# A fused attention and mixture-of-experts kernel: squared rows summed on GpSimd, bias steps for both sides at once, routing counts by rounding, and a written list of all steps

## The chip, the cores and the metric

The kernel runs on one core of one Trainium2 chip. The metric is the device time of one execution in microseconds (us), taken as the median of several runs. The profile is a trace of one execution; the lines "L503" and the like are lines of the kernel before. Engines are TensorE (PE, with its weight loads PEld), VectorE (DVE), ScalarE (ACT), GpSimd (POOL) and SyncE (SP), which issues most transfers; the others run in parallel and are tied by semaphores, and each works through its own instructions in the order in which the program gives them.

## The reference

Attention by random features, then one expert per token. There are 8 batches, 8 heads, 576 tokens, 64 dimensions, 128 features, 8 experts:

```
phi(x):  proj = x @ omega.T            # x scaled by 64**-0.25
         h = proj - sum(x*x)/2
         return exp(h - max(h)) / sqrt(128)
kv  = phi(k).T @ v ; z = sum(phi(k))
att = (phi(q) @ kv) / (phi(q) @ z + 1e-6)          # [4608, 512] in all
logits = att @ w_gate ;  e = argmax(logits)
gate = softmax(logits)[e] ; eom = sigmoid(att @ w_output_gate)[e]
out  = gate * eom * (relu(att @ w1[e]) @ w2[e])
```

The sum of squares of a token is the same for all its features, so it cancels against the maximum up to rounding; the kernel forms it all the same.

## The kernel before, in words

**Units.** The attention is cut into 32 units, four chunks of tokens (1152 tokens of two batches each) by eight heads. A unit loads k and q transposed (`xt32`, 576 KB) and values (`rawv`, 325 KB), and from unit 8 on k and q in natural order too (`xn`, 576 KB). It projects both sides (steps `pp`, three groups of 3 x 128 tokens, L503), takes the least value of each token (`mx`, L525, DVE), makes a bias from it (`nb`, L531, or L534 and L538), and takes the exponential with that bias (`ex`, L544, ACT). Then come the product of keys and values (`kv`, L640), halves of it in f16 (`kvs`, L660), its product with the gate weights (`kt`, `kg`, L678, L683), the transposed q features (`tq`/`th`/`tl`, L594, L599, L601 in the first eight units, a transposing DMA later), the numerator and denominator (`pn`, L714), the division (`xf`, L723 to L727) and two halves for the store (`xh`, L744, DVE; `xl`, L748, POOL). The gate logits are added up over the heads (`lga`, L766, POOL).

**The sum of squares.** In the first eight units ("whole" ones, `u < WHOLE`) the projection is in f32: `squares` writes the squares of the transposed data into `xn` (L480, POOL; L478, ACT for unit 0), and each group of `pp` adds six more matmuls for each six of the projection, squares times a tile `half` that holds a constant, so that PSUM holds projection and squares together. The bias is then one DVE instruction for each side and group (L531). From unit 8 on the projection is in f16 halves (`xhi`, `xlo`), ACT squares the natural data (`sqa`, L443), DVE sums it over the 64 dimensions (`sqr`, L448), and the bias is two instructions for each side and group (L534, L538).

**Routing and items.** When the eight heads of a chunk are done, `route`, `counts`, `ranks`, `places`, `gates` and `weigh` choose an expert and a place for each token, and `table`, `assign`, `lists`, `controls`, `pid`, `gi`, `advance` form lists of 128 tokens of one expert each ("items"). These are chains of small DVE instructions on 8 to 144 columns (L840 to L1189), with matmuls for the counts (L891 to L901) and lists (L1151). A rank is cut into slot and place by a cast to integer, a shift by 7 and a cast back. An item gathers its rows (`gx`, L1458, an indirect DMA from POOL), transposes them by DMA (`xt`, L1470), and runs the two layers (`hA`, `hB`, L1495, and `out`, L1526, PE, with `relu` L1502 ACT and `rest` L1506 DVE), scales (`os`, ACT) and stores (`put`, POOL). 38 items carry tokens here; where the expert changes, 4 MB of weights are brought and cut into halves (`sw`, L365 ACT, L369 DVE). The weights of a first expert, guessed, are cut early (`w0h`, `w0l`, the same lines).

**What sets the order.** All steps are registered with `plan.add`. A planner (`Plan.order`) plays them through once: of the ready steps it takes the one with the lowest rank among those that can start earliest, by costs that are written beside each step, with a model of DMA, of PSUM banks in two classes (5 for attention, 3 for items) and of TensorE at half speed after a quiet stretch. The result is the order of instructions on every engine; across engines semaphores hold.

Of the kernel before, what the change touches and what calls it, by code (L numbers as in the profile page):

```python
# [31 lines left out]
KEY = 64  # L32
KC = DM // P
# [40 lines left out]
SHIFT = {'hi': -1.4, 'lo': 0.3, 'sqa': 1.9, 'sqr': 2.3, 'T': 1.8, 'pp': 0.1, 'mx': 0.5, 'nb': -0.4, 'ex': -2.0, 'eh': -0.7, 'el': 1.4, 'eT': 0.4, 'kv': -0.5, 'kvs': -1.6, 'pn': -0.1, 'xf': -0.9, 'xh': 0.1, 'xl': 0.7, 'xT': -3.4, 'rows': -0.1, 'lg': -2.2, 'lga': -1.4, 'route': -1.8, 'gx': 1.7, 'xt': 1.0, 'hA': 0.7, 'hB': -1.1, 'relu': -2.1, 'rest': -0.6, 'out': 0.3, 'os': -0.1, 'put': 1.0}  # L74
# [25 lines left out]
C_END = C_DOWN + 1  # L100


def constants():
# [6 lines left out]
    c[:, C_ITEM:C_PART] = np.arange(NITEM)  # L110
# [4 lines left out]
    c[FEW:, C_DOWN] = -float(FEW)  # L115
    c[:, C_BOTH + 1 : C_UPPER : 2] = np.arange(NSC * NC) * P
# [3 lines left out]
    m[:, 2, :] = np.arange(P)  # L120
    m[:, 3, :] = np.eye(P)
    return c, m, np.eye(P, dtype=np.float32)


class Plan:

    HANDOFF, DRAIN, DMA_START, DMA_END, DMA_TURN, BACKLOG, LATE = 0.19, 0.13, 0.65, 0.95, 0.3, 2.5, 2.5
    TICK, ENOUGH = 3.413, 3060.0

    def __init__(self, banks):
        self.steps, self.seq, self.banks, self.bank_of = {}, 0, banks, {}
        self.part = 0
        self.makers, self.readers, self.bufs = {}, {}, {}  # L140

    def add(
        self, key, engine, cost, fn, after=(), rank=0.0, tiles=(), bank=None, frees=(), dma=0.0, turn=False, early=None, cols=None,
        lead={},
    ):


        assert key not in self.steps, key
        cost = cost if isinstance(cost, tuple) else (cost,) * len(engine)
        bank = [] if bank is None else bank if isinstance(bank, list) else [bank]  # L150
        s = dict(key=key, eng=engine, cost=cost, fn=fn, after=list(after), rank=(rank + SHIFT.get(key[0], 0.0), self.seq), bank=bank)
        s.update(frees=frees, dma=dma, turn=turn, tiles=sorted(set(tiles)), early=early, part=self.part, lead=lead)
        s["cols"] = cost[0] * 2400.0 if cols is None else cols
        self.seq += 1
        self.steps[key] = s
        for tag, i in s["tiles"]:
            self.readers.setdefault((tag, i), []).append(key)
# [18 lines left out]
    def lag(self, a, b):  # L176

        if a == b:
            return 0.0 if a == ("PE",) else self.DRAIN
        return 0.06 if b == ("SP",) else self.HANDOFF  # L180

    def order(self):
        steps = self.steps
        users, missing = {}, {}
        for k, s in steps.items():
            deps = set(s["after"])
            for tag, i in s["tiles"]:
                deps |= set(self.readers.get((tag, i - self.bufs[tag]), ()))
            s["deps"] = deps
            missing[k] = len(deps)  # L190
            for d in deps:
                assert d in steps, (k, d)
                users.setdefault(d, []).append(k)
        free_at = {"SP": 0.6, "DVE": 0.9, "POOL": 0.7, "ACT": 1.9, "PE": 0.1}
        bank_free = {b: 0.0 for b in range(sum(self.banks.values()))}
        bank_cls, b0 = {}, 0
        for c, n in self.banks.items():
            bank_cls[c] = range(b0, b0 + n)
            b0 += n
        bank_cls["e"] = range(b0)  # L200
        dma_free = 0.0
# [4 lines left out]
        while ready:  # L206
            best = None
            for k in ready:
# [9 lines left out]
                if best is None or t < best:  # L218
                    best = t
# [1462 lines left out]
```

## Time and profile before

| what | before |
|---|---|
| median of 3 runs (lowest to highest) | 659.51 us (658.62 to 664.33) |
| the profiled execution's own time | 659.44 us |
| its span (first to last instruction) | 657.6 us |
| matmul instructions | 8732 |
| DVE instructions busy | 1277 |
| read from and written to HBM | 83.86 MB, 19.30 MB |

The profile gives, for each group of instructions of one line and operation, the time during which it was busy, the mean duration of one, and the idle time of the engine before it with what ended it. Instructions of one engine overlap in their pipelines, so the mean of one is longer than its pitch (the distance from start to start); a table of windows gives the busy time of an engine without counting twice.

### The profile page before, as it was taken

What the parts mean: (1) busy time and instruction counts of PE and PEld (TensorE: products, weight loads), DVE (VectorE), ACT (ScalarE), POOL (GpSimd) and SP (SyncE); (2) the same over time, 40 slices, a digit from 0 to 9 for tenths busy, and PEclk for the clock granted to TensorE, in tenths of its full rate; (3) what the DMA queues carried; (4) which work ended last, traced back from release to release, by engine and by line L of the source; (5) the groups of instructions that cost most, each with busy time, mean ns of one, the idle gap of its engine ahead of it and who ended that gap; (6) DMA issues with size and microseconds to landing.
All of it is one profiled execution on the core that took longest, in us unless ns stands there. A gap on an engine that the chain in (4) does not pass through costs nothing. (4 is left out here: it accounts for less than half of the span.)

```text
span 657.6 us, 22358 instructions
## 1 busy us (share of the span) xinstructions
PE 608.3 (93%) x8732; PEld 474.6 (72%) x8732; DVE 426.8 (65%) x1277; ACT 412.0 (63%) x970; POOL 342.7 (52%) x235
## 2 busy tenths in 40 slices
PE   6999986799999899899989999999999999999983
PEld 6899975677777677677757777877768677677763
DVE  4899889876877897567697876752783430251043
ACT  5886797689888859788875788772521521341151
POOL 1343545569956958879574788955222122121202
PEclk9999988799999999999999999999999999999998
DMA  9544588998999989978999485867945846834460
GB/s 316 204 136 139 165 295 206 257 250 193 300 270 283 240 230 210 226 195 243 298 278 212 100 205 132 130 105 182 291 103 182 219 92 154 255 61 102 153 225 15
DMA packets 145894, 129.09 MB, mean 196 GB/s; under 512 B 104270, under 2 KB 127440, under 8 KB 144464
## 3 DMA queue, kind: packets, MB, share of 16 engines
q1 hardware_dynamic: 139760, 107.45, 64.6%
q0 software_dynamic: 5984, 19.72, 9.2%
q8 instruction: 85, 1.39, 0.9%
q14 instruction: 65, 0.53, 0.3%
HBM read 83.86 MB, written 19.30 MB: 157 GB/s over the span
## 5 line engine op out<-in xcount | busy, mean ns | idle before, releaser
L1495 PE MATMUL ph<-xt,w1h 128*128 128x128 f16 (+1 forms) x2432 | 206.1, 218 | 3.5 <-issue 1.7
L1495 PE MATMUL ph<-xt,w1l 128*128 128x128 f16 (+1 forms) x1216 | 201.4, 217 | 2.2 <-DVE w1l L369 0.9
L1495 PEld LDWEIGHTS <-w1h 128*128 128x128 f16 x2432 | 181.9, 98 | 12.3 <-issue 5.8
L544 ACT ACTIVATE ef<-pp,nb 128x128 f32<-128x128 f32 x576 | 162.9, 392 | 42.0 <-DVE nb L538 33.1
L1506 DVE SCALAR_TENSOR_TENSOR hl<-ph,hh 128x512 f16<-128x512 f32 (+1 forms) x76 | 50.6, 666 | 121.9 <-ACTq L1424 74.9
L567 POOL TENSOR_TENSOR es<-ef,es 128x1152 f16<-128x1152 f32 x44 | 104.9, 2392 | 36.0 <-ACT es L565 21.1
L525 DVE TENSOR_REDUCE pp<-pp 128x3 f32<-128x384 f32 x192 | 102.7, 557 | 30.0 <-PE pp L503 26.2
L1495 PEld LDWEIGHTS <-w1l 128*128 128x128 f16 x1216 | 118.6, 98 | 2.9 <-issue 1.5
L1458 POOL DMA_INDIRECT gx<-rows,gi x38 | 39.9, 1049 | 138.0 <-ACT os L1581 103.1
L1526 PE MATMUL po<-w2h,hl 128*128 128x512 f16 x280 | 106.7, 381 | 2.4 <-DVEq L1424 1.3
L1526 PE MATMUL po<-w2h,hh 128*128 128x512 f16 x280 | 107.1, 382 | 0.0
L1526 PE MATMUL po<-w2l,hh 128*128 128x512 f16 x280 | 106.6, 381 | 0.0
L1502 ACT ACTIVATE hh<-ph 128x512 f16<-128x512 f32 (+1 forms) x76 | 44.3, 583 | 87.5 <-PE ph L1495 71.3
L1526 PEld LDWEIGHTS <-hh 128*128 128x128 f16 x560 | 51.7, 99 | 57.1 <-issue 2.7
L1581 ACT ACTIVATE os<-po,gx 128x512 f32<-128x512 f32 (+1 forms) x36 | 24.5, 682 | 65.6 <-PE po L1526 63.7
L437 POOL TENSOR_TENSOR xlo<-xt,xhi 128x1152 f16<-128x1152 f32 x24 | 57.2, 2385 | 13.5 <-ACT xhi L430 12.2
L565 ACT CAST es<-ef 128x1152 f16<-128x1152 f32 x44 | 51.3, 1177 | 6.3 <-DMA et<-es 5.9
L714 PE MATMUL pn<-kvs,et 128*128 128x81 f16 (+1 forms) x960 | 46.4, 205 | 7.7 <-DVE kvs L701 2.1
L1526 PEld LDWEIGHTS <-hl 128*128 128x128 f16 x280 | 27.5, 98 | 36.0 <-DVE hl L1506 1.9
L714 PEld LDWEIGHTS <-et 128*128 128x128 f16 (+1 forms) x960 | 40.1, 102 | 16.5 <-issue 5.6
L748 POOL TENSOR_TENSOR xs<-xf,xs 128x576 f16<-128x576 f32 x32 | 43.2, 1351 | 10.2 <-DVE xs L744 9.3
L503 PE MATMUL pp<-omh,xhi 64*128 64x128 f16 x432 | 42.6, 221 | 6.3 <-DVE xf L727 3.1
(185 smaller groups left out, 1048.6 us busy)
## 6 DMA issues: line engine op xcount, KB each, us to landing
r<-w SPq DMA_DIRECT2D x10, 2048.0 KB
xt<-kqt SPq DMA_DIRECT2D x32, 576.0 KB
xn<-kqn SPq DMA_DIRECT2D x24, 576.0 KB
rawv<-v SPq DMA_DIRECT2D x32, 325.0 KB
rows<-xs SPq DMA_DIRECT2D x16, 576.0 KB
r<-w SPq DMA_DIRECT2D x8, 512.0 KB
ef<-w SPq DMA_DIRECT2D x2, 512.0 KB
et<-w SPq DMA_DIRECT2D x2, 512.0 KB
```

What stands on the lines that cost most here:

```text
L437: lambda t0=t0, t1=t1: nc.gpsimd.tensor_tensor(out=xl(u)[:, t0:t1], in0=xt32(u)[:, t0:t1], in1=xh(u)[:, t0:t1], op=ALU.subtract),
L503: nc.tensor.matmul(banks["pp", 2 * u + i, g][:, c, :], x[r, t], w[r, :], start=(a == 0), stop=(a == len(ops) - 1))
L525: nc.vector.tensor_reduce(out=pp[:, 3, 0:3], in_=pp[:, 0:3, :], op=ALU.min, axis=AX.X)
L544: nc.scalar.activation(ef(n)[:, c, :], banks["pp", n, g][:, c % 3, :], AF.Exp, bias=nb(n)[:, c : c + 1], scale=-SK)
L565: nc.scalar.copy(es(slot_es(n))[:, 0], ef(n))
L567: nc.gpsimd.tensor_tensor(out=es(slot_es(n))[:, 1], in0=ef(n), in1=es(slot_es(n))[:, 0], op=ALU.subtract)
L714: nc.tensor.matmul(pn[lo:hi, c - c0, :], a[:, c, lo:hi], w[:, b, :], start=(i == 0), stop=(i == len(ops) - 1))
L748: nc.gpsimd.tensor_tensor(out=x[:, :, P + o : P + o + D], in0=xf(u)[:, :, 0:D], in1=x[:, :, o : o + D], op=ALU.subtract)
L1495: nc.tensor.matmul(ph[:, f4, 0:w_], w[qd][:, kk, fo : fo + P], xt(n)[:, x, 0:w_], start=(a == 0), stop=(a == 3 * KC - 1))
L1502: nc.scalar.activation(hh(n)[:, sl, 0:w_], banks["ph", n, g][:, :, 0:w_], AF.Relu)
L1506: nc.vector.scalar_tensor_tensor(out=hl(n)[:, sl, 0:w_], in0=banks["ph", n, g][:, :, 0:w_], scalar=0.0, in1=hh(n)[:, sl, 0:w_], op0=ALU.ma ...
L1526: nc.tensor.matmul(po, x(n)[:, f, :], w[f // 2][:, f % 2, :], start=(f == 0 and a == 0), stop=(f == FC - 1 and a == 2))
```

## The change

**Squares.** The matmuls with `half` are gone. Every unit loads `xn` in natural order. Unit 0 squares it on ACT and sums it on DVE as later units do. Units 1 to 7 form the squares on POOL (1152 columns) and fold them there: 576, 288 and 144 columns of additions, then a scaling of 144 columns; DVE sums the last eight for each token (18 sums out of 144 columns).

**Bias.** `nb` now holds both sides. After the two `mx` of a group, two DVE instructions make the bias of k and q together (6 columns). The exponentials of k wait for the `mx` of q as well.

**Routing.** Counts and ranks are kept as tokens less 63.5, and a rank is rounded to whole slots by adding and subtracting 1.5 * 2^23 * 128; the counts so far come in by two more f32 matmuls (`ident` times `cnt`); several copies are gone. For one chunk and its list the DVE chain has 23 instructions where it had 29 in `ranks` (4, now 3), `places` (5, now 4), `table` (9, now 7), `assign` (8, now 7) and `lists` (3, now 2); the copy `cp` has moved from `lists` into `places`.

**Order.** The planner, its ranks and the table of shifts are gone. `ORDER` lists all 3333 steps by number and `BANKS` the PSUM bank of each use, any of the eight. A number is the place of a step's `plan.add` call: 0 to 30 are constants and first weights, 31 to 85 are unit 0, then 59 steps for each of the units 1 to 7, 51 for each of 8 to 11, 55 for each of 12 to 31, 1803 on the stores of rows, 1819 on the routing, 1906 on the lists and flags, 2112 on the items (16 steps each for the first 25, then 29). So 2118 is the first layer of item 0 (`hA`), 2116 its gather, 1824 `counts` of chunk 0, 710 to 712 `pp` of unit 12, 659 to 661 `pp` of unit 11, 683 and 684 `kv` of unit 11.

```diff
+ORDER = """
+31 0 32 86 87 5 36 34 37 33 1 7 39 38 40 35 45 41 95 89 51 42 43 44 2 146 145 10 4 13 52 98 53 99 54 46 47 48 90 55 49
...
+1807 631 813 670 671 675 676 677 873 634 761 2118 672 678 683 2119 679 667 673 684 874 2120 635 636 710 711 685 637
...
     def order(self):
-        steps = self.steps
...
+        numbered = list(self.steps.values())
+        out = [numbered[int(x)] for x in ORDER.split()]
...
+    def squares(u, R):
+
+        if u == 0:
+            natural_sums(u, R, ("ACT",))
+            return
+        x = lambda: sqt(u)
+
+        def fold(w):
+            if w == D:
+                nc.gpsimd.tensor_tensor(out=x(), in0=xn(u), in1=xn(u), op=ALU.mult)
+            elif not w:
+                nc.gpsimd.tensor_scalar(x()[:, :, :, 0 : D // 8], x()[:, :, :, 0 : D // 8], SK * SK / 2.0, None, ALU.mult)
+            else:
+                nc.gpsimd.tensor_tensor(out=x()[:, :, :, 0:w], in0=x()[:, :, :, 0:w], in1=x()[:, :, :, w : 2 * w], op=ALU.add)
+
+        after = [("ld", "n", u)]
+        for w, cost in ((D, 2.3), (D // 2, 1.2), (D // 4, 0.7), (D // 8, 0.4), (0, 0.3)):
+            plan.add(
+                ("sqa", u, w), ("POOL",), cost, lambda w=w: fold(w), after=after, rank=R - 15, tiles=[("xn", u), ("sqt", u)]
+            )
+            after = [("sqa", u, w)]
+        plan.add(
+            ("sqr", u), ("DVE",), 0.3,
+            lambda: nc.vector.tensor_reduce(
+                out=sqs(u).rearrange("p i c -> p c i"), in_=x()[:, :, :, 0 : D // 8], op=ALU.add, axis=AX.X
+            ),
...
                 if whole:
-                    ops = [(xt32(u), omf), (xsq(), half)]
+                    ops = [(xt32(u), omf)]
...
-            before_ = [("lo", u, x), ("const", "omh")]
+            before_ = [("ld", "t", u) if whole else ("lo", u, x), ("const", "omh")]
...
+        spare = lambda g, at: banks["pp", 2 * u, g][:, 3, at : at + 6].rearrange("p (i c) -> p i c", i=2)
+
+        def least(i, g):
+            nc.vector.tensor_reduce(
+                out=spare(g, 0)[:, i], in_=banks["pp", 2 * u + i, g][:, 0:3, :], op=ALU.min, axis=AX.X
+            )
+
+        def bias(g):
+            c = slice(3 * g, 3 * g + 3)
+            sq = sqs(u)[:, :, c]
+            nc.vector.scalar_tensor_tensor(
+                out=spare(g, 6), in0=spare(g, 0), scalar=SK, in1=sq, op0=ALU.mult, op1=ALU.add
+            )
+            yield
+            nc.vector.scalar_tensor_tensor(
+                out=nb(u)[:, :, c], in0=spare(g, 6), scalar=LIFT, in1=sq, op0=ALU.add, op1=ALU.subtract
+            )
...
-        nc.tensor.matmul(pos[:, 0:NC, :], tri, one, start=True, stop=False)
+        nc.tensor.matmul(pos[:, 0:NC, :], ident, cnt.unsqueeze(1).broadcast_to([P, NC, NE]), start=True, stop=False)
+        nc.tensor.matmul(pos[:, 0:NC, :], tri, one, start=False, stop=False)
...
-        ri = inner(j, "ri", [NC], I32)
-        nc.vector.tensor_copy(ri, rank)
-        yield
-        nc.vector.tensor_scalar(ri, ri, 7, None, ALU.arith_shift_right)
-        yield
-        nc.vector.tensor_copy(key, ri)
-        yield
-        nc.vector.scalar_tensor_tensor(out=rank, in0=key, scalar=-float(P), in1=rank, op0=ALU.mult, op1=ALU.add)
...
+        nc.vector.tensor_scalar(key, rank, ROUND, ROUND, ALU.add, ALU.subtract)
+        yield
+        nc.vector.tensor_tensor(out=rank, in0=rank, in1=key, op=ALU.subtract)
```

More of the change, by code (lines that the diff above doesn't have):

```diff
@@ new lines, in order @@
+        numbered = list(self.steps.values())
+        out = [numbered[int(x)] for x in ORDER.split()]
+        assert len(out) == len({s["key"] for s in out}) == len(numbered)
+        done, taken, free = set(), iter(BANKS.replace("\n", "")), set(range(8))
+        for s in out:
+            before = set(s["after"])
+            for tag, i in s["tiles"]:
+                before |= set(self.readers.get((tag, i - self.bufs[tag]), ()))
+            assert before <= done, s["key"]
+            done.add(s["key"])
+            for _, name, _ in s["bank"]:
+                self.bank_of[name] = int(next(taken))
+                free.remove(self.bank_of[name])
+            for name in s["frees"]:
+                free.add(self.bank_of[name])
@@ L459, in unit @@
         whole = u < WHOLE
-        for nm, t, src, rank in (("t", xt32, kqt, R - 30), ("n", xn, kqn, R - 22))[: 1 if whole else 2]:
+        for nm, t, src, rank in (("t", xt32, kqt, R - 30), ("n", xn, kqn, R - 22)):
             plan.add(
@@ new lines, in unit @@
+                ("pp", u, g), ("PE",), 0.66 if whole else 0.6, lambda g=g: project(g), after=before_, rank=R,
+                tiles=[("xt32", u)] if whole else [("xhi", u), ("xlo", u)],
+                bank=[(cls, ("pp", 2 * u + i, g), [4, M]) for i in range(2)], cols=1536.0 if whole else 1152.0,
+            )
+        spare = lambda g, at: banks["pp", 2 * u, g][:, 3, at : at + 6].rearrange("p (i c) -> p i c", i=2)
[3 more added lines that the diff above has]
+            )
@@ new lines, in unit @@
+        for g in range(G):
+            for i in range(2):
+                plan.add(
+                    ("mx", 2 * u + i, g), ("DVE",), 0.47, lambda i=i, g=g: least(i, g), rank=R + 0.5 * i,
+                    after=[("mx", 2 * u, g)] if i else [("pp", u, g)],
+                )
+            plan.chain(
+                ("nb", u, g), ("DVE",), (0.1, 0.1), lambda g=g: bias(g), rank=R + 0.5,
+                after=[("mx", 2 * u + 1, g)] + [("sqr", u)], tiles=[("nb", u), ("sqs", u)],
+            )
+            for i in range(2):
+                plan.add(
+                    ("ex", 2 * u + i, g), ("ACT",), 0.76, lambda i=i, g=g: exps(i, g), after=[("nb", u, g)], rank=R + i,
+                    tiles=[("nb", u), ("ef", 2 * u + i)], frees=[("pp", 2 * u + i, g)],
@@ L968, in table @@
         t["off"] = off
-        nc.vector.tensor_tensor(out=off[:, 0, :], in0=done[:, 0, :], in1=start, op=ALU.subtract)
+        nc.vector.scalar_tensor_tensor(
+            out=off[:, 0, :], in0=done, scalar=ROUND, in1=start, op0=ALU.subtract, op1=ALU.subtract
+        )
         yield
```

284 lines of the change are left out of this document (83 added, 201 removed), and 127 rows, old and new, of the table ORDER.

## The prediction

> **What bounds the kernel now.** I read the page's first lines, then a table of windows, then TensorE's and VectorE's instructions in order of time in the stages that the change touches, then groups and waits.
>
> ```profile
> span 657.6 us, 22358 instructions
> PE 608.3 (93%) x8732; PEld 474.6 (72%) x8732; DVE 426.8 (65%) x1277; ACT 412.0 (63%) x970; POOL 342.7 (52%) x235
> ```
>
> TensorE is busy for 93% of the span, so at first sight its work is the time. The windows (columns: length, busy time of PE, PEld, DVE, ACT, POOL, granted clock, DMA share, GB/s) say more:
>
> ```profile
> 0.00:10.00 10.00, 4.91 (x46) 4.91 (x48) 2.21 (x10) 3.38 (x7) 2.31 (x5) 1.00 0.83 284
> 10.00:80.00 70.00, 69.32 (x945) 63.14 (x945) 62.20 (x175) 56.86 (x180) 26.89 (x19) 1.00 0.54 177
> 80.00:131.00 51.00, 38.52 (x534) 33.66 (x531) 46.46 (x188) 38.78 (x112) 26.50 (x19) 0.83 0.94 253
> 131.00:440.00 309.00, 294.72 (x4689) 225.31 (x4688) 232.69 (x748) 243.96 (x571) 236.80 (x152) 0.99 0.88 217
> 440.00:640.00 200.00, 193.27 (x2385) 141.39 (x2385) 77.10 (x153) 64.67 (x98) 46.34 (x41) 1.00 0.64 168
> 640.00:657.60 17.60, 7.60 (x150) 6.19 (x146) 6.16 (x7) 4.32 (x7) 3.86 (x2) 0.79 0.06 15
> ```
>
> Up to 80 us, the eight whole units, TensorE never pauses, but VectorE is at 62.20 of 70 and ACT at 56.86. From 80 to 131 TensorE has 12.5 us idle and a clock of 0.83, while VectorE is at 46.46 of 51: it closes chunk 0 and serves the next units. The first item starts at 131:
>
> ```profile
> 115.37 1.16 POOL L1458 DMA_INDIRECT gx<-rows,gi  x1 [0.32 <-DVE rt L1121]
> 130.93 0.27 PE L1495 MATMUL ph<-xt,w1h 128*128 128x128 f16 x2
> ```
>
> After that TensorE is bound by its work: 495.6 of 526.6 us up to the end. So two things set the end: when the items can start, which hangs on VectorE, and how much TensorE work and idle time is left then. TensorE work taken out before 131 us counts only as far as the start of the items moves with it.
>
> **The squares.** Rows of one whole unit (start, duration):
>
> ```profile
> 44.84 2.48 PE L640 MATMUL kv<-rawv,ef 128*128 128x130 f32 x20
> ...
> 48.23 0.39 PE L503 MATMUL pp<-half,xn 64*128 64x128 f32 x4
> 48.45 0.39 PE L503 MATMUL pp<-omf,xt 64*128 64x128 f32 x4
> ...
> 74.08 2.48 PE L640 MATMUL kv<-rawv,ef 128*128 128x130 f32 x20
> ```
>
> From `kv` to `kv` three units take 29.24 us, 9.75 each. One burst with `half` has a pitch of 0.22 us; nine a unit are 2.0 us, 16 us for eight units. TensorE alone would then need 7.75 us a unit. The same three units by engine:
>
> ```profile
> sum 29.24, PE 29.24 PEld 26.75 DVE 27.01 ACT 20.29 POOL 11.93; mean PE 9.75 PEld 8.92 DVE 9.00 ACT 6.76 POOL 3.98
> ```
>
> VectorE has 9.00 us in the 9.75. It becomes the bound, and it gets more: the sum of 144 columns, 0.32 us by the row of that shape in the lists (0.2 to 0.3 as a pitch; I take 0.30). The bias of whole units stays at two instructions a group.
>
> ```profile
> L1002 DVE TENSOR_REDUCE rt<-rt 128x18 f32<-128x144 f32 x1 | 0.3, 316 | 0.0
> L480 POOL TENSOR_TENSOR xn<-xt 128x1152 f32<-128x1152 f32 x7 | 15.1, 2153 | 26.8 <-DMA xt<-kqt 26.8
> L748 POOL TENSOR_TENSOR xs<-xf,xs 128x576 f16<-128x576 f32 x32 | 43.2, 1351 | 10.2 <-DVE xs L744 9.3 <-DVEq L1419 0.4 <-DVE nb L531 0.4
> L766 POOL TENSOR_TENSOR lga<-lga,xf 128x144 f32<-128x144 f32 x24 | 14.2, 590 | 38.9 <-DVE xf L727 22.3 <-DVE nb L538 5.8 <-DVE nb L531 5.5
> L764 POOL COPY lga<-xf 128x144 f32<-128x144 f32 x4 | 1.4, 343 | 4.7 <-DVE xf L727 4.7
> ```
>
> GpSimd's chain: 2.15 for 1152 columns, 1.35 for 576, about 0.9 for 288 (between 1.35 and 0.59), 0.59 for 144, 0.34 for the scaling: 5.3 us instead of 2.15. A unit then has 3.98 + 3.2 = 7.2 us of GpSimd in 9.75, so the chain is covered if it runs a unit ahead; queued behind it are `xl` and `lga` of the unit before, for whose rows and logits nobody waits until chunk 0 closes. But GpSimd and VectorE disturb each other:
>
> ```profile
> 26.49 2.10 POOL L480 TENSOR_TENSOR xn<-xt 128x1152 f32<-128x1152 f32 x1
> 26.54 2.40 DVE L744 CAST xs<-xf 128x576 f16<-128x576 f32 x1
> ...
> 47.00 0.60 DVE L744 CAST xs<-xf 128x576 f16<-128x576 f32 x1
> ...
> 58.15 1.28 POOL L748 TENSOR_TENSOR xs<-xf,xs 128x576 f16<-128x576 f32 x1
> 58.55 1.96 DVE L369 SCALAR_TENSOR_TENSOR w2l<-r,w2h 128x1024 f16<-128x1024 f32 x1
> ...
> 63.55 1.21 DVE L369 SCALAR_TENSOR_TENSOR w2l<-r,w2h 128x1024 f16<-128x1024 f32 x1
> ...
> L744 DVE CAST xs<-xf 128x576 f16<-128x576 f32 x32 | 30.4, 949 | 0.2
> ```
>
> A cast that takes 0.60 us undisturbed took 2.40, until GpSimd's instruction was over; its mean is 0.95, so it waits 0.35. An instruction that meets another at random waits, on average, the sum of the squared lengths over twice the period: (2.15² + 1.28² + 0.59²) / 19.5 = 0.34, which fits. With the new chain the squares sum to 9.7, over 19.5 it is 0.50: 0.16 more. Two VectorE instructions a unit are of this kind, the cast and one weight piece `w0l` (1.96 beside GpSimd, 1.21 without): +0.3. VectorE then needs 9.00 + 0.30 + 0.3 = 9.6 of 9.75 us. The 16 us of TensorE work are covered almost whole; what can be won is VectorE's idle time in this stage, 7.8 us from 10 to 80, of which its new work takes 8 x 0.6 = 4.8. I take **-3**; ends -5 (no new waits: 7.8 less 8 x 0.3) and, with GpSimd always in the way, a rival below. The Trainium skill, page "SBUF — State Buffer", section "Who interferes with whom", calls this an exclusive lock of a port pair, held for a whole instruction, for casts and for VectorE instructions with two SBUF inputs, and says that reductions never take part; the rows above agree for cast and weight piece. By that rule the new sum (`sqr`) never waits, and the sum stays as it is.
>
> The other pieces of this edit: the added loads, 576 KB for each of eight units, find the DMA engines at 0.54 of their time between 10 and 80 us; nothing, as long as SP's queue does not stand: a load of `xn` waits for the buffer that GpSimd's first product of two units earlier frees, and the loads of `rawv` and `xt` queue behind it. At the start, unit 0's bias waits for load, square and sum, about as long as it waited for its squares' matmuls: nothing either way. In TensorE's idle time the clock may drop, a rival below.
>
> **The bias.** From unit 8 on a group has two VectorE instructions fewer:
>
> ```profile
> L534 DVE SCALAR_TENSOR_TENSOR pp<-pp,sqs 128x3 f32<-128x3 f32 x144 | 21.9, 162 | 0.5 <-DVEq L1419 0.2
> L538 DVE SCALAR_TENSOR_TENSOR nb<-pp,sqs 128x3 f32<-128x3 f32 x144 | 21.1, 155 | 2.7 <-ACT ef L544 1.1
> L525 DVE TENSOR_REDUCE pp<-pp 128x3 f32<-128x384 f32 x192 | 102.7, 557 | 30.0 <-PE pp L503 26.2
> L503 PE MATMUL pp<-omh,xhi 64*128 64x128 f16 x78 | 9.3, 230 | 4.8 <-DVE xf L727 1.9 <-ACT ef L544 1.5 <-DVE ahead L1140 0.6
> ```
>
> The last row counts the f16 projections before the first item: 78, six a group, 13 groups. 13 x 0.317 = 4.1 us of VectorE work go from the stage up to 131 us, and 59 x 0.317 = 18.7 after it. The price, k's exponentials waiting for q's `mx`, is one such instruction, 0.56 us of latency a group, covered by other groups' work.
>
> **The routing.** Six fewer instructions of about 0.17 us for chunk 0:
>
> ```profile
> L925 DVE TENSOR_SCALAR rt<-rt 128x9 int32<-128x9 int32 x4 | 0.7, 174 | 0.1
> L683 PE MATMUL kv<-wgr,kvf 128*128 128x32 f32 x64 | 12.1, 271 | 1.3 <-ACT kvf L689 1.3
> ```
>
> That is 1.0 us of VectorE. Four times two f32 matmuls more on TensorE: by the f32 row of 32 columns 0.27 us each or less, 2.2 in all if none overlaps; I take **+1** (ends 0.3 and 2). Before the first item this gives 4.1 + 1.0 = 5.1 us less work on an engine that is at 91% there; but between the first gather and the first item lie 15.6 us in which a DMA latency could decide as well. I take **-3**, between 0 and -5.
>
> **The list.** By its numbers the first layer of item 0 (2118) stands behind `pp` of unit 11 and ahead of 683 and 684 (`kv` of unit 11) and 710 (unit 12); in the trace unit 12's first group is ahead of it (24 + 13 groups). Some 3 us of TensorE work (2.48 and a group) move behind the start; its sum stays. Behind 131 us VectorE loses 18.7 us and three more routings' 3 us. TensorE's waits there, longest in total:
>
> ```profile
> PE po L1518 <- DVE hl L1506: 2.8, 3, 1.1
> PE ph L1495 <- issue: 2.6, 6, 0.7
> PE pn L714 <- DVE kvs L701: 1.8, 1, 1.8
> ```
>
> Its idle time from 131 to 440 is 309 - 294.7 = 14.3 us, in many small pieces; of all its waits behind 131 us about half are put down to VectorE. A lighter VectorE and another order may take some: **-4**, between 0 and -14 (an order without a pause). The last 217 us hold items alone and keep their 6.7 us of idle time and the ramp at the end. No row shows how good the list is; it could also add pauses.
>
> **The sum**, against the profiled execution's own 659.44 us (0.07 us below the median of the runs, so no correction): -3 - 3 + 1 - 4 = -9, so 650.4; I say **650 us**.
>
> **Rivals.** *Covered*: VectorE's relief goes where nobody waits, the units run at the old 9.75 us, and only small things remain: -2, so 657. For it: TensorE is bound by work after 131 us whatever VectorE does. Against it: VectorE's 91% before the first item. *TensorE's work decides*: stage one is limited by TensorE after all since the weight pieces move out of it, the item start moves by most of the 16 us, and the list takes half of the 14.3 us: -15 - 7 = -22, so 637. For it: VectorE's 9.6 contain a weight piece of 1.2. Against it: that piece must be done before the first item anyway. *Slower by GpSimd's hold on VectorE*: if every cast meets a full product, it waits 1.8 instead of 0.35, and a weight piece up to 0.75 more: +2.2 a unit, VectorE at 9.00 + 0.3 + 2.2 = 11.5, so 8 x 1.75 = +14, with the other terms' -6: +8, so 667. It decides once the extra waiting is above 0.45 us a unit (9.75 - 9.3), and beats the other terms above 1.2. For it: 2.40 was seen; against it: the new instructions are mostly shorter. *Slower by the clock*: TensorE at 7.75 of 9.7 us a unit is 80% busy, and the stage with 75% had 0.83; below a clock of 0.80 TensorE is again above 9.6, and at 0.70 it needs 11.1: 8 x 1.4 - 6 = +5, so 664. The Trainium skill, page "TensorE: Matmul & The Clock Gate", section "Part 1: The HAM clock gate", knows only full and half rate, half after an idle window of about 3.4 us; no window of this stage would be idle by that, and by it this rival falls away.
>
> **The numbers.** Forecast 0.46, covered 0.28, TensorE's work 0.13, GpSimd's hold 0.08, the clock 0.05. A measurement of this kernel tells about 1%, 6.6 us, from no change: faster means below 652.9. The third case and four fifths of the first are faster, with a little of the second: 0.56; slower 0.11; the rest, 0.33, within 1%. The likeliest case alone spans 643 to 656; the range takes in most of the others: 636 to 664.
>
> **What would show it.** Right: whole units at 9.3 to 9.7 us with VectorE at 95% or more and TensorE pausing; the first item at 123 to 127 us; casts (L744) in that stage at 1.0 to 1.2 us in the mean; PE's idle time between first item and 440 near 10 us. Wrong: units near 8 us (VectorE was no bound), casts at 2 us, a granted clock below 0.8 before 80 us, or a TensorE that stands ahead of item 0 or of the exponentials.

## The result, and the profile after

The kernel became slower: median of 4 runs 679.83 us (676.4 to 683.21) against 659.37 us for the kernel before in the same comparison, a ratio of 1.0281 with a 95% interval of 1.0230 to 1.0332. The prediction said 650 us, range 636 to 664. The profiled execution took 677.2 us, its span is 675.4. Each ratio in this document leaves out runs of a slower state, over 1.5% above the fastest of their kernel, so it can differ a little from the ratio of the medians.

The first lines of the page, after:

```profile
span 675.4 us, 21674 instructions
PE 608.3 (90%) x8460; PEld 469.0 (69%) x8460; DVE 428.8 (63%) x1116; ACT 414.0 (61%) x968; POOL 362.6 (54%) x263
```

TensorE is busy for 608.3 us as before, although 272 matmuls are gone (288 with `half` less 16 new ones of the routing), 16 us by the pitch of before. Its idle time went from 49.3 us (657.6 less 608.3) to 67.1, and that difference of 17.8 us is the whole growth of the span. The table of windows, after (length, busy time of PE, PEld, DVE, ACT, POOL, granted clock, DMA share, GB/s):

```profile
0.00:10.00 10.00, 4.65 (x48) 4.46 (x48) 3.31 (x9) 2.44 (x2) 0.19 (x4) 1.00 0.80 273
10.00:80.00 70.00, 60.88 (x645) 53.20 (x643) 60.55 (x180) 56.06 (x176) 47.47 (x44) 0.88 0.73 247
80.00:131.00 51.00, 33.53 (x446) 28.89 (x445) 45.54 (x135) 33.42 (x95) 26.08 (x18) 0.81 0.81 222
131.00:440.00 309.00, 297.47 (x4594) 227.76 (x4593) 224.65 (x608) 238.01 (x552) 220.55 (x141) 0.98 0.89 213
440.00:640.00 200.00, 189.72 (x2361) 137.85 (x2358) 82.54 (x174) 72.13 (x129) 62.69 (x54) 0.99 0.59 159
640.00:657.60 17.60, 15.25 (x236) 11.45 (x235) 4.80 (x7) 5.95 (x9) 2.57 (x3) 1.00 0.87 255
657.60:675.40 17.80, 6.82 (x150) 5.36 (x146) 7.45 (x8) 5.99 (x9) 3.00 (x2) 0.87 0.06 14
```

Read it against the rows of before. From 10 to 80 us TensorE now pauses for 9.1 us (before 0.7) and its clock is 0.88 instead of 1.00; from 80 to 131 it pauses 17.5 us (before 12.5). VectorE has hardly less to do there: 109.4 us up to 131 against 110.9. The clock fell in stretches in which TensorE was busy most of the time. In windows of 5 us it is 0.72 and 0.60 from 10 to 20 us, 0.58 and 0.73 from 25 to 35, 0.66 from 55 to 60, and 1.00 in the others up to 80; pauses of 2.72, 2.01 and 0.91 us, the three longest of the stage, end at 12.94, 26.88 and 55.90. The Trainium skill, page "TensorE: Matmul & The Clock Gate", describes something like this in its section "A second HAM failure mode: psum-queue depth-cycling": in a kernel that cycles through PSUM banks, short pauses between groups of matmuls are frequent enough to bring half rate time and again. The trace agrees that short pauses are enough (0.88 with 60.88 of 70 us busy); that the banks have a part in it is not shown. The page's table in "Part 1: The HAM clock gate", which I had used alone, has half rate after an idle window of about 3.4 us, and no pause of this stage is longer than 2.72.

The first item, after: its gather, and the first matmul of its first layer. A row has start, duration, engine, line and instruction; in brackets stands how long the engine was idle before it, and what ended that.

```profile
123.87 1.17 POOL L1524 DMA_INDIRECT gx<-rows,gi  x1 [11.03 <-DVE ctl L1137]
...
139.15 0.27 PE L1561 MATMUL ph<-xt,w1h 128*128 128x128 f16 x2
```

8.2 us later than the 130.93 of before, instead of 4 to 8 us earlier. Three whole units, from one product of keys and values to the same product three units on:

```profile
48.71 2.51 PE L707 MATMUL kv<-rawv,ef 128*128 128x130 f32 x20
...
78.20 2.51 PE L707 MATMUL kv<-rawv,ef 128*128 128x130 f32 x20
```

29.49 us, 9.83 a unit, no shorter than the 9.75 of before: TensorE is busy for 25.90 of the 29.49 us and VectorE for 26.76, where before TensorE was busy for all of the time. The groups of the edit's instructions (mean ns of one, then the idle time before them):

```profile
L591 DVE TENSOR_REDUCE pp<-pp 128x3 f32<-128x384 f32 x192 | 105.9, 560 | 34.5 <-PE pp L572 21.2 <-remote 2.9 <-PE pn L781 2.8
L598 DVE SCALAR_TENSOR_TENSOR pp<-pp,sqs 128x6 f32<-128x6 f32 x96 | 16.0, 167 | 1.7
L602 DVE SCALAR_TENSOR_TENSOR nb<-pp,sqs 128x6 f32<-128x6 f32 x96 | 14.9, 158 | 1.8 <-DVEq L1485 0.2 <-issue 0.2
L531 DVE TENSOR_REDUCE sqs<-sqt 128x18 f32<-128x144 f32 x7 | 2.1, 295 | 0.8 <-POOL sqt L519 0.7
L517 POOL TENSOR_TENSOR sqt<-xn 128x1152 f32<-128x1152 f32 x7 | 14.9, 2122 | 18.0 <-DMA xn<-kqn 10.4 <-DVE sqs L531 4.5 <-DVE kvs L727 2.5
L521 POOL TENSOR_TENSOR sqt<-sqt 128x576 f32<-128x576 f32 (+2 forms) x21 | 19.8, 941 | 1.5
L519 POOL TENSOR_SCALAR sqt<-sqt 128x144 f32<-128x144 f32 x7 | 4.0, 572 | 0.6
```

Each new instruction takes about what was forecast: the chain on GpSimd is 2.12 + 3 x 0.94 + 0.57 = 5.5 us (5.3 forecast), the sum on VectorE 0.30, a bias step on six columns no more than one on three. So it is not the price of the instructions. TensorE's waits, after (total, times, longest):

```profile
PE kv L750 <- ACT kvf L756: 6.5, 5, 4.5
...
PE pn L781 <- ACT ef L608: 5.1, 3, 2.4
...
PE pp L572 <- DVE ahead L1206: 3.5, 1, 3.5
PE pp L572 <- DVE et L668: 3.2, 3, 2.0
PE pn L781 <- DVE kvs L768: 2.8, 2, 2.1
PE tq L661 <- DVE nb L602: 2.7, 1, 2.7
```

Five of these six rows stand for one to three waits each. TensorE waits for copies and exponentials of ScalarE (`kvf`, `ef`), for a bias (`nb`) and for what stands late in VectorE's queue; each such wait holds a step of the attention.

### The profile page after: what moved, and what is told of

Same layout as the page of the kernel before. It is cut to its first block, busy times and chain, and to the rows that moved or that the text cites. A ratio compares the mean times of both kernels' runs of the same rounds, so it can differ in the third digit from the quotient of the medians.

```text
span 675.4 us, 21674 instructions
## 1 busy us (share of the span) xinstructions
PE 608.3 (90%) x8460; PEld 469.0 (69%) x8460; DVE 428.8 (63%) x1116; ACT 414.0 (61%) x968; POOL 362.6 (54%) x263
## 5 line engine op out<-in xcount | busy, mean ns | idle before, releaser
L608 ACT ACTIVATE ef<-pp,nb 128x128 f32<-128x128 f32 x576 | 164.8, 387 | 59.8 <-DVE nb L602 48.0
L591 DVE TENSOR_REDUCE pp<-pp 128x3 f32<-128x384 f32 x192 | 105.9, 560 | 34.5 <-PE pp L572 21.2
L815 POOL TENSOR_TENSOR xs<-xf,xs 128x576 f16<-128x576 f32 x32 | 41.0, 1284 | 40.8 <-DVE xs L811 23.6
L1647 ACT ACTIVATE os<-po,gx 128x512 f32<-128x512 f32 (+1 forms) x36 | 24.7, 685 | 57.8 <-PE po L1592 57.3
L781 PE MATMUL pn<-kvs,et 128*128 128x81 f16 (+1 forms) x960 | 48.7, 213 | 8.9 <-ACT ef L608 5.1
L781 PEld LDWEIGHTS <-et 128*128 128x128 f16 (+1 forms) x960 | 42.0, 107 | 15.7 <-issue 9.8
```

The lines of the kernel that those rows point to most:

```text
L591: nc.vector.tensor_reduce(out=spare(g, 0)[:, i], in_=banks["pp", 2 * u + i, g][:, 0:3, :], op=ALU.min, axis=AX.X)
L608: nc.scalar.activation(ef(2 * u + i)[:, c, :], banks["pp", 2 * u + i, g][:, c % 3, :], AF.Exp, bias=nb(u)[:, i, c : c + 1], scale=-SK)
L781: nc.tensor.matmul(pn[lo:hi, c - c0, :], a[:, c, lo:hi], w[:, b, :], start=(i == 0), stop=(i == len(ops) - 1))
```

## The experiments

Two theories stood at first. **Operations**: the new operations cost time at their places (the bias for both sides makes k's exponentials wait, the first stage gets later). **Order**: the order before is fitted to the operations before, and any other order or set of operations loses 1 to 2%. A third question was whether TensorE's removed work counted at all. All kernels in one table; times are medians, a ratio is against runs of before in the same comparison (their medians went from 657.0 to 663.4 us, so 659.37 is the divisor of the second row alone), and the other columns come from one profiled execution each: first `relu`, the gather of item 25 (the first item behind chunk 3's routing), and the span.

| kernel | us | ratio (95%) | first relu | gather 25 | span | span less gather 25 |
|---|---|---|---|---|---|---|
| before | 659.37 | 1 | 134.4 | 500.8 | 657.6 | 156.8 |
| after | 679.83 | 1.0281 (1.0230 to 1.0332) | 142.1 | 514.5 | 675.4 | 160.9 |
| e1 new operations, old planner | 669.00 | 1.0200 (1.0142 to 1.0257) | 138.9 | 510.5 | 666.8 | 156.3 |
| e2 old operations, written list | 673.80 | 1.0300 (1.0232 to 1.0368) | 157.8 | 517.6 | 672.0 | 154.4 |
| e3 squares only, old planner | 671.73 | 1.0239 (1.0180 to 1.0299) | 133.2 | 510.6 | 666.2 | 155.6 |
| e4 bias only, old planner | 665.58 | 1.0154 (1.0106 to 1.0202) | 134.3 | 509.0 | 665.1 | 156.1 |
| e5 old operations, other tie | 670.94 | 1.0194 (1.0141 to 1.0247) | 135.6 | 511.5 | 666.0 | 154.5 |
| e6 after, projection twice | 681.84 | 1.0329 (1.0292 to 1.0365) | 142.4 | 522.7 | 684.1 | 161.4 |
| e7 e1, bias by side in whole units | 692.21 | 1.0511 (1.0449 to 1.0573) | 134.3 | 532.2 | 689.1 | 156.9 |
| e8 planner, then list | 679.74 | 1.0311 (1.0277 to 1.0345) | 140.9 | 513.5 | 674.4 | 160.9 |
| e9 before, chunk 3 held for 9 us | 672.27 | 1.0160 (1.0081 to 1.0240) | 135.3 | 513.6 | 670.3 | 156.7 |
| e10 before, chunk 3 held for 18 us | 682.80 | 1.0283 (1.0189 to 1.0378) | 135.1 | 526.5 | 684.2 | 157.7 |
| e11 new operations, refitted | 675.48 | 1.0198 (1.0150 to 1.0245) | 138.8 | 511.8 | 669.5 | 157.7 |
| e12 e7, refitted | 668.34 | 1.0102 (1.0046 to 1.0157) | 119.3 | 508.0 | 665.5 | 157.5 |
| e13 old operations, refitted | 670.36 | 1.0113 (1.0069 to 1.0157) | 135.6 | 513.8 | 670.8 | 157.0 |
| e14 routing only, old places | 663.21 | 1.0058 (1.0014 to 1.0102) | 136.1 | 506.8 | 664.1 | 157.3 |
| e15 bias from unit 8 only, old places | 669.07 | 1.0112 (1.0056 to 1.0169) | 138.2 | 510.2 | 669.2 | 159.0 |

**The parts, with the old planner and with the list (e1 to e4).** e1 takes the kernel after and gives it back the planner:

```diff
-    plan = Plan()
+    plan = Plan({"a": 5, "b": 3})
...
-        out = [numbered[int(x)] for x in ORDER.split()]
+            k = min((k for k in ready if steps[k]["est"] <= best + TIE), key=lambda k: steps[k]["rank"])
```

> All new operations (squares folded on GpSimd, bias for both sides, routing by rounding), but the order made by the old planner with its old ranks, shifts and bank classes instead of the written list. Theory A, the list costs the time: between 645 and 660 us, first item at or before 131 us. Theory B, the operations cost it (the start with its added loads and the chain on GpSimd, latency ahead of the exponentials): 672 us or more, and the second unit's kv again some 6 us later than before. Theory C, both in part: 662 to 670 us.

e2 is the kernel before with its own operations at the places that the list gives to their counterparts (32 of its 3333 steps put later, where what they need was not there yet; the list after has 3208 steps, not the 3333 named under "The change"):

```diff
-    plan = Plan({"a": 5, "b": 3})
+    plan = Plan()
...
+        out = self.settled([numbered[int(x)] for x in ORDER.split()])
```

> All operations as before, but in the order of the written list with its banks: each old step stands where its counterpart stands in the list (squares of a whole unit ahead of its projection, the bias steps of both sides where the joint ones stand, longer routing chains spread over the shorter ones); 32 steps of 3333 are put later since they would stand ahead of what they need. Theory A, the list costs the time: 672 us or more, with the items alone at the end (from the 25th item on) again some 6 us longer than before. Theory B, the operations cost it: 655 to 662 us.

e3 makes only the edit of the squares, with the old planner and the bias of each side by itself:

```diff
-                    ops = [(xt32(u), omf), (xsq(), half)]
+                    ops = [(xt32(u), omf)]
...
+            squares(u, R)
```

> The kernel before with the squares' edit alone (no squares in the projection's matmuls, squares folded on GpSimd in units 1 to 7, a sum on VectorE, the bias of whole units in two instructions for each side as in later units), old planner. Theory A (the squares' edit is about neutral, VectorE holds the first stage): 652 to 662 us. Theory B (the edit costs the start): 664 us or more, unit 1's kv some 5 us later.

e4 makes only the edit of the bias, in all units, with the old planner:

```diff
+            plan.chain(
+                ("nb", u, g), ("DVE",), (0.1,) if whole else (0.1, 0.1), lambda g=g: bias(g), rank=R + 0.5,
```

> The kernel before with the bias of both sides made together and nothing else (whole units: one instruction for both sides instead of two; later units: two instead of four), old planner. Theory A (VectorE's relief is worth 2 to 6 us): 653 to 658 us. Rival (k's exponentials waiting for q's least value cost more than the instructions saved): 661 us or more.

Every one of them is slower than before, by 1.5 to 3%. e1 fell between its theories (C, both in part), e2 where the list costs the time, though its items at the end took no longer (154.4 us behind the gather of item 25), e3 and e4 where the edit costs. But the parts do not add up: squares and bias together (e1, with the routing) lose 2.0%, the squares alone 2.4, the bias alone 1.5. Parts that lose by themselves and no more in company point to the order that each kernel got, not to a price.

**Order alone (e5).** One number of the kernel before, the planner's tie: steps that can start within this many us of the earliest compete by rank.

```diff
-TIE = 0.1
+TIE = 0.12
```

> The kernel before with all its own operations, and one number of the planner changed: it takes the lowest rank among steps that can start within 0.12 us of the earliest, not 0.10. The planner's own play-through ends at 597.7 us with it and at 596.6 without, so by its own reckoning the order is as good. Theory 'order': the order before is fitted to these operations on this chip, and any other order costs 0.5 to 2%, whatever the operations: 661 to 670 us. Rival 'operations': the loss of the change comes from what its operations cost at their places, another order of equal reckoning is neutral: 654 to 660 us, and the interval of the ratio holds 1.

1.0194. The same operations, in an order that the planner itself reckons nearly as good, lose 1.9%: about as much as a single edit. The rival falls. So a replanned kernel cannot price an edit to better than about 2%, and that holds for e1, e3, e4 and e7.

**Does TensorE's removed work count (e6)?**

```diff
-                    ops = [(xt32(u), omf)]
+                    ops = [(xt32(u), omf)] * 2
...
-                            banks["pp", 2 * u + i, g][:, c, :], x[r, t], w[r, :], start=(a == 0), stop=(a == len(ops) - 1)
+                            banks["pp", 2 * u + i, g][:, c, :], x[r, t], w[r, :], start=whole or a == 0, stop=whole or a == len(ops) - 1
```

> The kernel after, with each f32 projection of the first eight units issued twice, the second time over the first: as many matmuls as the squares had, put back on TensorE, 16 us at the pitch of before, with no other step touched (the work is useless, the result the same). Theory 'clock': TensorE's removed work only came back as half clock, so that the kernel with it is no slower, 674 to 683 us, its granted clock back at 0.97 or above from 0.959, first item at 139 to 142 us (after: 139.15). Theory 'work': TensorE's load counts in the first stage, so the first item moves by 5 us or more and the end with it: 685 to 695 us.

681.84 us, and the intervals of the two ratios overlap: 16 us of work put back on TensorE move the time by 0.5% at the middle, 1.4% at the most. The first relu moves by 0.3 us; the gather of item 0 comes 4.8 us later (128.64 against 123.87). The windows of e6:

```profile
10.00:80.00 70.00, 64.10 (x811) 57.90 (x807) 56.54 (x164) 52.53 (x166) 47.20 (x44) 0.95 0.66 227
80.00:131.00 51.00, 37.20 (x529) 32.70 (x531) 46.60 (x148) 36.48 (x101) 22.21 (x15) 0.83 0.81 229
```

TensorE's idle time up to 131 us falls by 7 us (31.9 to 24.7) and the clock from 10 to 80 us rises from 0.88 to 0.95: a part of the added work goes into idle time, and with it goes a better clock. Theory 'clock' is right about the time, but the clock did not rise to 0.97 over the whole span (0.962), so it explains only a part. TensorE's load alone is not what sets the first item.

**The joint bias in the first stage (e7).** In whole units each side gets its own two instructions and its exponentials wait for its own `mx` alone:

```diff
+            if whole:
+                for i in range(2):
+                    n = 2 * u + i
+                    plan.add(("mx", n, g), ("DVE",), 0.47, lambda i=i, g=g: one_least(i, g), rank=R + i, after=[("pp", u, g)])
...
+                        ("ex", n, g), ("ACT",), 0.76, lambda i=i, g=g: exps(i, g), after=[("nb", n, g, "one")], rank=R + i,
```

> The new operations in the order of the old planner (669.0 us, first relu at 138.85), but in the first eight units the bias is made for k and q each by itself, two small instructions a side, so that k's exponentials don't wait for q's least value; from unit 8 on it is joint as in the kernel after. Theory 'latency': the joint bias is what makes the first stage late, so the first relu comes at 133 to 135 us and the time falls by as much, to 663 to 666 us. Rival 'end decides': the first stage does get earlier, but the end doesn't, since chunk 3's routing and the last chunk's items set it: 667 to 671 us.

Both are wrong about the time by a wide margin, and that taught most. The first relu of e1, and then that of e7:

```profile
138.85 0.62 ACT L1520 ACTIVATE hh<-ph 128x512 f16<-128x512 f32 x1
```

```profile
134.28 0.60 ACT L1550 ACTIVATE hh<-ph 128x512 f16<-128x512 f32 x1
```

The first relu comes 4.6 us earlier without the join, as 'latency' said. One pair of replanned kernels is weak evidence, but all kernels that make both the squares' edit and the joint bias in whole units start late (e1, e11, e8, after and e6, first relu at 138.8 to 142.4), and all with the squares' edit and the bias by side start earlier (e3, e7 and e12, 133.2, 134.3 and 119.3). Where TensorE still does the squares, the join shows no such price: e4 has its first relu at 134.3, before at 134.4. And yet e7 ends 22 us later than e1 (by the profiled spans), and nearly all of that is there when item 25's gather leaves:

```profile
532.17 0.99 POOL L1506 DMA_INDIRECT gx<-rows,gi  x1 [4.10 <-DMA ef<-w]
```

e1's gather left at 510.46. A better start, followed by an order that happens to be bad, ends worse.

**Where the list loses (e8).** The planner orders the new operations up to the first layer of item 0, the list from there on:

```diff
+            if ("hA", 0) in done:
+                k = min((k for k in ready if steps[k]["est"] < 1e8), key=wanted.get)
+            else:
                 k = min((k for k in ready if steps[k]["est"] <= best + TIE), key=lambda k: steps[k]["rank"])
```

> The kernel after's operations, ordered by the old planner up to the first layer of item 0, and by the written list from there on (banks by the planner's play, any of eight). Theory 'start': the list loses in front of the first item alone (first relu 142.08 against 138.85 with the planner), so this kernel is at 668 to 673 us. Rival 'rest': what the list loses against the planner's order lies behind the first item, in the last chunk's items (items 27 to 37 took 121.7 us in the kernel after and 115.7 with the planner): 675 to 680 us.

679.74, the 'rest'. What the list loses against the planner lies mainly behind the first item: of the 7.6 us between the profiled spans of e8 and e1, 2.1 are there at the first relu, 3.0 at the gather of item 25, and 4.6 come behind it. After, e6 and e8, which end in the list's order, need 161 us behind that gather, the planner's kernels 154 to 158. It is no proof, since e2, the old operations at the list's places, needs 154, and since e8's order and banks are a third order, not e1's up to the first item.

**Is a late chunk 3 the cause or a sign (e9, e10)?** In all kernels the end follows the gather of item 25 by 154 to 161 us, while the gather itself moves by 31. The kernel before, with the last unit's gate columns multiplied by 1.0 on GpSimd, 14 or 28 times:

```diff
             mine, total = xf(u)[:, :, D:], lga(j)
+            if u == NSC * H - 1:
+                for _ in range(28):
+                    nc.gpsimd.tensor_scalar(mine, mine, 1.0, None, ALU.mult)
```

> The kernel before, same operations in the same order, but between the division of the last unit and the last sum of its gate logits GpSimd multiplies those 144 columns by 1.0 fourteen times, some 0.57 us each by the scaling row of the kernel after: chunk 3's routing comes 8 us later and nothing else is asked to move. Theory 'routing sets the end': in the kernel before, item 25's gather leaves at 500.84 and its first relu comes 17.5 us behind it; in the kernel with the new operations in the planner's order it comes 11.2 us behind. So there are some 6 us of slack and 8 us of delay cost 1 to 4 us: 659 to 663 us. Rival 'elastic': TensorE has other items to do and the end does not hang on this routing: within 2 us of before.

> The same with twenty-eight such instructions, 16 us later. Theory 'routing sets the end': delay less 6 us of slack, so 8 to 12 us slower than before, 666 to 671 us, with TensorE pausing between 505 and 540 us; that is what the kernels e1 to e5 lost, whose routing of chunk 3 was 11 to 22 us late. Rival 'elastic': under 3 us slower, and then the lateness of chunk 3's routing in the other kernels is a sign and not the cause.

9 and 19 us slower by the medians, more than either theory had. The instructions held chunk 3 for 9.06 and 18.19 us, a little more than asked. GpSimd's row and VectorE's queue in e10 show why so little of it was absorbed:

```profile
472.47 18.19 POOL L765 TENSOR_SCALAR xf<-xf 128x144 f32<-128x144 f32 x28 [3.35 <-DVE xf L727]
...
471.32 0.97 DVE L727 TENSOR_TENSOR xf<-pn,den 128x400 f32<-128x400 f32 x2
490.69 0.32 DVE L771 TENSOR_TENSOR rt<-lga,xf 128x144 f32<-128x144 f32 x1 [18.40 <-POOL xf L765]
490.92 0.49 DVE L744 CAST xs<-xf 128x576 f16<-128x576 f32 x1
491.32 0.22 DVE L843 TENSOR_REDUCE r_top<-rt 128x9 f32<-128x72 f32 x1
491.45 5.70 DVE L369 SCALAR_TENSOR_TENSOR w1l<-r,w1h 128x1024 f16<-128x1024 f32 x4
```

VectorE stands for 18.40 us in front of the sum of the gate logits. Queued behind it are four weight pieces `w1l`, whose data have nothing to do with the routing, and TensorE's next item waits for them (its pause ahead of `ph` with `w1l` is 17.6 us long; in e9 VectorE stands for 9.28 us and TensorE for 8.47). So there was no slack of 6 us to use up: an instruction that is late holds all that the order put behind it on its engine, and the delay goes to TensorE one for one. The experiment does not separate 'routing sets the end' from 'the queue behind it stands'; it shows that a late instruction at this place costs about its whole lateness, even where TensorE has other items. A constant distance from gather 25 to the end is no proof of a cause either: an order fixes how much of TensorE's work is left at that point.

**An order fitted to the new operations (e11, e12) and the control (e13).** The table of shifts (what the planner adds to the rank of each kind of step) and the tie were fitted anew by thousands of play-throughs, to e1's kernel, to e7's and to the kernel before. Nearly all entries of the table change; the tie becomes 0.12, 0.10 and 0.07. In e11:

```diff
-TIE = 0.1
+TIE = 0.12
```

> The new operations in the order of the old planner, with its table of shifts and the tie (0.12) fitted anew to them by some thousands of play-throughs: the play-through puts the last second-layer step of item 36 at 592.8 us (594.0 for the kernel before, 603.7 for the new operations with the old table) and chunk 3's counts at 429.1 (427.7 and 445.2). Theory 'order': the loss belongs to the fit of order and operations, so the refitted order takes back most of the 2%: within 0.7% of before, 654 to 664 us. Rival 'operations': the new operations lose by themselves, and this stays at 1.02 or above, 669 to 680 us. In either case the end follows the gather of item 25 by 154 to 161 us.

> The same refit for the new operations with the bias of the first eight units made side by side, the kernel that was slowest (1.051): item 0's first layer at 107.1 us in the play-through (117.0 for the kernel before), counts of chunk 3 at 436.1, item 36 at 591.4. Theory 'order': the 5% go, and with the earlier start it ends between 645 and 662 us; first relu at 125 to 131 us. Rival 'operations': 670 us or more.

> The control: the kernel before's own operations, its table fitted anew by the same number of play-throughs, which then end item 36 at 589.1 us instead of 594.0. Theory 'order, fitted on the chip': a better play-through doesn't make the chip faster, since the table before was chosen on it: 656 to 672 us. Rival 'the play-through is right': 5 us faster than before, 651 to 656 us.

e11 stays at 1.0198: the refit gave it nothing. e12 goes from 1.0511 to 1.0102, and the control, old operations in an order that the play-through holds for 5 us better, is at 1.0113, the same, as 'order, fitted on the chip' had it. So with orders made in the same way, the new operations (with the bias by side in whole units) and the old ones are level, and neither reaches the kernel before. 'Operations' holds for e11, where the joint bias in the first stage stays. In e12 most of the 5% goes, as 'order' said, but its 668.34 us lie between the two ranges, and its start is earlier than the 125 to 131 us forecast. e12 also shows the edit of the squares doing what it was said to do. Its units and windows, and the sum over the three units:

```profile
41.96 2.48 PE L689 MATMUL kv<-rawv,ef 128*128 128x130 f32 x20
...
66.79 2.51 PE L689 MATMUL kv<-rawv,ef 128*128 128x130 f32 x20
```

```profile
10.00:80.00 70.00, 63.08 (x744) 55.09 (x741) 65.88 (x239) 61.00 (x195) 55.81 (x50) 1.00 0.84 286
80.00:131.00 51.00, 34.98 (x503) 30.16 (x502) 43.65 (x147) 35.07 (x100) 24.50 (x16) 0.80 0.78 188
131.00:440.00 309.00, 294.33 (x4540) 224.05 (x4537) 220.21 (x598) 237.49 (x548) 236.13 (x149) 0.99 0.83 217
...
sum 24.83, PE 24.83 PEld 21.81 DVE 23.88 ACT 20.95 POOL 21.51; mean PE 8.28 PEld 7.27 DVE 7.96 ACT 6.98 POOL 7.17
```

24.83 us for three units, 8.28 each. TensorE is busy in all of them and is the bound again; VectorE needs 7.96 us a unit. The first relu comes at 119.3 instead of 134.4, 15 us earlier. But from 80 to 131 TensorE then idles for 16.0 us at a clock of 0.80, and the gather of item 25 is 7 us later than before. The early start was not kept.

**Single edits at the old places (e14, e15).** Here nothing is planned anew: the order of the kernel before is written out, step by step and bank by bank, with one set of operations changed in place.

```diff
-    plan = Plan({"a": 5, "b": 3})
+    plan = Plan()
...
+        out = [numbered[int(x)] for x in ORDER.split()]
```

> The kernel before with the routing edit alone (counts less 63.5, rounding by a large constant, two more f32 matmuls a chunk), its steps written out at the places, and with the banks, that the old order gave them; nothing else differs. Theory 'small and off the path': six fewer small VectorE instructions a chunk against two matmuls, within 0.7% of before, 655 to 664 us. Rival 'any edit of the operations costs': 666 us or more, as in every kernel so far that touched an operation.

> The kernel before with the joint bias from unit 8 on alone, again at the places of the old order: q's least value stands right ahead of the bias at k's place, two VectorE instructions a group are gone, the first eight units are as before. Theory 'latency': k's exponentials wait for q's least value in each group of 24 units, in an order that leaves no cover for it: 664 to 673 us. Rival 'work' (the prediction's term): 18 to 23 us less VectorE work, so level or faster, 652 to 660 us.

Both came as their first theories said. The routing edit gains nothing: 1.0058, an interval of 1.0014 to 1.0102, with medians of 663.21 and 662.74 us. The joint bias from unit 8 on costs 1.1% at these places although it takes 144 VectorE instructions away: first relu 138.2, where kernels with the operations of before in the same order up to there have 134.4, 135.3 and 135.1 (before, e9, e10). The rival 'work', which was my term, falls. The joint bias of the whole units and the squares were not timed at the old places.

## Why the prediction was wrong, step by step

- **"The price, k's exponentials waiting for q's `mx`, is one such instruction, 0.56 us of latency a group, covered by other groups' work."** This step failed. It is not covered. At the old places the join from unit 8 on makes the first relu 2.9 to 3.8 us later (e15; units 8 to 11 have 12 groups, so 0.24 to 0.32 us of the 0.56 a group) and the whole kernel 1.1% slower, where I had 18.7 us of VectorE work saved behind 131 us. For the whole units e1 against e7 gives 4.6 us for 24 groups, 0.19 a group, but in two different orders, and e4 shows none of it. So the join has no fixed price: what comes through depends on the order and on which engine bounds the stage.
- **The routing**, 1.0 us less VectorE work before the first item and +1 on TensorE: too small to matter, and it did not help (e14).
- **The squares, -3.** In another order, with the bias by side, the term was too small for the stage: units of 8.28 us in e12, first item 15 us earlier, as the rival "TensorE's work decides" had it for the stage. My 9.6 us a unit for VectorE rested on 9.00 of before, and the three units that I measured hold three weight pieces:

```profile
L369 DVE SCALAR_TENSOR_TENSOR w2l<-r,w2h 128x1024 f16<-128x1024 f32 x3 | 4.4, 1460 | 0.0
```

In e12's three units there is none, and VectorE needs 7.96 us a unit; that the pieces move away is what the rival had named. In the kernel after none of the gain is seen: its three units hold three such pieces again, and its exponentials wait for the joint bias. How much each of the two takes is not shown.

- **"So two things set the end: when the items can start, which hangs on VectorE, and how much TensorE work and idle time is left then."** This step failed as well, and it is the deeper one. e12 starts 15 us earlier and ends 8 us later (profiled spans); idle time and low clock behind the start swallow the gain. What my sum did not look at is chunk 3. "The last 217 us hold items alone" is a wrong reading of before: the last attention step and the indices of chunk 3, for which item 25 waits, lie in these 217 us:

```profile
461.08 1.40 PE L714 MATMUL pn<-kvs,et 128*128 128x81 f16 x30
...
500.38 0.18 DVE L1181 TENSOR_TENSOR gi<-r_gid,r_other 128x24 uint32<-128x24 f32 x1
```

In the kernel after that last `pn` starts at 485.46, 24 us later, and the indices come at 513.50, 13 us later. Holding this stretch of before for 9 and 18 us cost 9 and 19 (e9, e10).

- **"A lighter VectorE and another order may take some"**, -4, between 0 and -14. The sign was wrong. The list costs 0.8% against the planner with the same operations (1.0281 and 1.0200, intervals overlapping; e8, at 1.0311 clear of e1, puts most of it behind the first item), and the old operations at the list's places lose 3.0% (e2). I had written that no row shows how good the list is, and still gave no loss a place among the ends.
- **Missing altogether**: that another order by itself could lose, with the operations of before. e5 moves the time by 1.9% with one number, the refit of e13 by 1.1%; the first is more than my whole forecast gain.
- **The rivals.** "GpSimd's hold" did not come: up to 100 us the casts (L811) take 0.48 us each. "The clock" came in part, 0.88 before 80 us, and not by the load alone: e1 has 0.93 with 57.70 us busy, e12 1.00 with 63.08. "Covered" was right about TensorE's 16 us (e6) and wrong that nothing else would be lost.
- **The signs I named**: units at 9.83 us (9.3 to 9.7 said), first item at 139.15 (123 to 127 said), casts at 0.48 (1.0 to 1.2 said), TensorE's idle time from 131 to 440 us 11.5 (near 10 said; it is the one that came).

What stays open: which pairs of steps make an order good, and so how the 2.8% divide among the list, the join and the rest. The gather of item 25 tells how an order ended, not why its chunk 3 was late, and e9 and e10 delay VectorE's queue along with the routing. No version here beats the kernel before.

## What to carry to other kernels

Where all engines run from one fixed order, price an edit at the old places first, one edit at a time, and change the order by itself as a control: here a change of one planner number weighed as much as any edit. Work taken from an engine counts only where that engine ends the wait; look for the step that releases the last stage (here the gather of item 25) and ask of every edit whether it moves that. An instruction saved at the price of a join can be a loss: here the join from unit 8 on cost 1.1% although every engine had other work.

## What of the hardware was not expected

- Less than the full clock was granted in stretches where TensorE was busy: 0.88 from 10 to 80 us with 60.88 of 70 us busy and no pause over 2.8 us, against 1.00 with 69.32 busy before; in e6 0.95 with 64.10 busy and no pause over 1.3 us. No threshold comes out of these runs: e12 keeps 1.00 with 63.08 busy and pauses up to 1.4 us.
- The kernel before varies from execution to execution by more than the first runs showed: 652.44 to 669.63 us over all comparisons, which is why the ratios above carry intervals of about half a per cent to a per cent to each side. In e10 the last `pn`, ahead of the delay and in the same order of instructions, was 7 us later than in the profile of before (468.33 against 461.08). Two waits for a transposing DMA of the q features, 8 us together, stand in e10:

```profile
323.08 2.15 PE L714 MATMUL pn<-kvs,et 128*128 128x81 f16 x28 [5.33 <-DMA et<-es]
...
363.93 1.35 PE L714 MATMUL pn<-kvs,et 128*128 128x81 f16 x18 [2.92 <-DMA et<-es]
```

In before all such waits behind 131 us come to 1.1 us; e9, whose last `pn` is 3.6 us late, has one of 4.34 at 324.52. Why the transfer landed later is not shown. So a single gather in the table can be read to some 7 us only.

- GpSimd's scaling of 144 columns takes 0.57 us in the mean, more than a copy of the same width (0.34 in the rows of before; after the median is 0.35, and one of four took 1.30) and close to an addition (0.59 before, 0.51 after).
